# One level of Strassen's algorithm in a channel mixer's up-projection, in fp32, woven with the down-projection of the pair before

## The chip, the cores and the metric

One NeuronCore of a Trainium2 chip; the program runs on that core alone. The metric is the device time of one execution in microseconds, lower is better.

## The reference, cut to what matters

```python
batch, seq, dim = (8, 3008, 256)             # x
d_tok, d_ch = (256, 1536)                    # weights are float64 inputs
# attention part: a filter in the frequency domain along seq
X = np.fft.rfft(x, axis=1)
y = np.fft.irfft(X * (filt_r + 1j * filt_i)[None], n=x.shape[1], axis=1)
# mixer part, on y
xt = y.transpose(0, 2, 1)
h = np.maximum(xt @ w_tok1, 0.0) @ w_tok2    # token mixing
u = y + h.transpose(0, 2, 1)
h2 = np.maximum(u @ w_ch1, 0.0) @ w_ch2      # channel mixing: up (256 -> 1536), relu, down (1536 -> 256)
out = (u + h2).astype(np.float32)
```

The channel mixing is the bulk of the arithmetic. Everything is computed in fp32.

## The kernel before

The filter is done as a two-stage Fourier transform on TensorE: first-stage units (`a_unit`), second-stage units with the multiplication by the filter on VectorE (`b_unit`) and their inverses (`bi_unit`). The filter of the next batch or pair of batches runs beside the mixer of the present one: it is a Python generator, and the mixer's loop calls for one of its steps at every second half pair (every half pair in the first batch). In the traces an engine takes up its work in the order in which it was issued (an instance from ScalarE stands below, at 228 us).

The mixer works on six column blocks of 512 (the last 448) for each batch, and in each on six pairs of hidden tiles; 8 x 6 x 6 = 288 pairs. The down-projection already uses Strassen's algorithm: seven half-width products for eight.

```python
    def hidden(ut, jt, w, hh):
        ps = bank("pg")
        for c in range(DH):
            nc.tensor.matmul(ps[:, 0:w], wc1[:, c, ts(jt, P)], ut[:, c, 0:w],
                             start=(c == 0), stop=(c == DH - 1))
        nc.scalar.activation(out=hh[:, jt % 2, 0:w], in_=ps[:, 0:w], func=AF.Relu)
    def sums(hh, w):
        hw = w // 2
        t = tp.tile([P, 4, 256], FP32, tag="t", name="t")
        v = nc.vector.tensor_tensor
        v(out=t[:, 0:2, 0:hw], in0=hh[:, :, hw:w], in1=hh[:, 0, 0:w].rearrange("p (s n) -> p s n", s=2), op=ALU.subtract)
        v(out=t[:, 2, 0:hw], in0=t[:, 1, 0:hw], in1=hh[:, 0, 0:hw], op=ALU.add)
        v(out=t[:, 3, 0:hw], in0=t[:, 2, 0:hw], in1=hh[:, 1, 0:hw], op=ALU.subtract)
        return t
    def products(m, jp, hh, t, po):
        w = width(m)
        hw = w // 2
        if jp == 0:
            for i in range(4):
                po.append(bank("po%d" % i).rearrange("p (s n) -> p s n", s=2))
        b11, b21, b22 = hh[:, 0, 0:hw], hh[:, 1, 0:hw], hh[:, 1, hw:w]
        t1, t3, t2, t4_ = (t[:, i, 0:hw] for i in range(4))
        todo = ((1, b21), (2, b22)), ((3, t4_), (6, t1)), ((0, b11), (5, t2)), ((4, t3),)
        for i, parts in enumerate(todo):
            for j, (n, mov) in enumerate(parts):
                nc.tensor.matmul(po[i][:, j, 0:hw], wc2[:, jp, n, :], mov, start=(jp == 0 and j == 0),
                                 stop=(jp == JP - 1 and j == len(parts) - 1))
    def finish(b, m, ut, po):
        w = width(m)
        hw = w // 2
        us = ut[:, :, 0:w].rearrange("p d (s n) -> p d s n", s=2)
        u2, u3 = (sp.tile([P, 256], FP32, tag=n, name=n)[:, 0:hw] for n in ("u2", "u3"))
        def add(out, x0, x1):
            nc.vector.tensor_tensor(out=out, in0=x0, in1=x1, op=ALU.add)
        p23, p45, p16, p7 = (v[:, :, 0:hw] for v in po)
        add(us[:, 0], p23, us[:, 0])
        add(us[:, 1], p45, us[:, 1])
        add(us[:, 0, 1], p45[:, 1], us[:, 0, 1])
        nc.scalar.copy(out=u3, in_=p16[:, 0])
        add(u2, p16[:, 1], u3)
        add(us[:, 0, 0], us[:, 0, 0], u3)
        add(u3, p7[:, 0], u2)
        add(us[:, 0, 1], us[:, 0, 1], u2)
        add(us[:, 1], us[:, 1], u3.unsqueeze(1).to_broadcast([P, 2, hw]))
        # ... (cut: two transposes on VectorE, 16 stores)
```

The loop over the pairs:

```python
    def mix(b, next_ready, convert):
        wait = [0]
        pos, hhs, sms = {}, {}, {}
        more = b + 1 < B
        items = [(m, jp) for m in range(MT) for jp in range(JP)]
        n = len(items)
        for i in range(n + 1):
            for half in range(2):
                next(convert, None)
                if i < n:
                    m, jp = items[i]
                    if half == 0:
                        hhs[i] = hp.tile([P, 2, 512], FP32, tag="hh", name="hh")
                    hidden(uts[b, m], 2 * jp + half, width(m), hhs[i])
                    if half == 1:
                        sms[i] = sums(hhs[i], width(m))
                        if m + 1 < MT and jp in (2, 3):
                            u_part(b, m + 1, jp - 2)
                            if jp == 3:
                                wait.append(m + 1)
                        if more and i == n - 2:
                            h1s[b + 1] = token_relu(token_sums(b + 1))
                        if more and i == n - 1:
                            u_part(b + 1, 0, 0)
                elif more and half == 0:
                    u_part(b + 1, 0, 1)
                if half == 1 and i >= 1:
                    m, jp = items[i - 1]
                    products(m, jp, hhs.pop(i - 1), sms.pop(i - 1), pos.setdefault(m, []))
                    if jp == JP - 1:
                        finish(b, m, uts[b, m], pos[m])
                if more and next_ready():
                    for c in wait:
                        t4_load(b + 1, c)
                    wait.clear()
                yield
```

The up-projection of a pair is two `hidden` calls: four full-width matmuls, the activation by ScalarE straight from PSUM. The float64 weights are converted by `rounded`, one ScalarE and five or six VectorE operations for each 128x512 piece. Ten pieces (the "late" ones) are converted by `next(convert, None)` inside the first five pairs of the first batch.

```python
    def rounded(st, n, parts, late=False):
        words = [st.bitcast(t).rearrange("p (n w) -> p n w", w=2)[:, 0:n] for t in (U32, FP32)]
        lo, hi, hi_f = words[0][:, :, 0], words[0][:, :, 1], words[1][:, :, 1]
        if late:
            top = pp.tile([P, 512], FP32, tag="p1", name="top")[:, 0:n]
            rest = pp.tile([P, 512], FP32, tag="p2", name="rest")[:, 0:n]
        else:
            both = hp.tile([P, 2, 512], FP32, tag="hh", name="both")
            top, rest = both[:, 0, 0:n], both[:, 1, 0:n]
        top_i, rest_i = top.bitcast(U32), rest.bitcast(U32)
        nc.scalar.activation(out=top, in_=hi_f, func=AF.Copy, scale=2.0 ** -112)
        nc.vector.tensor_scalar(out=top_i, in0=top_i, scalar1=3, scalar2=None, op0=ALU.logical_shift_left)
        nc.vector.scalar_tensor_tensor(out=top_i, in0=hi, scalar=0x80000000, in1=top_i,
                                       op0=ALU.bitwise_and, op1=ALU.bitwise_or)
        nc.vector.tensor_scalar(out=rest_i, in0=top_i, scalar1=0xFF800000, scalar2=None, op0=ALU.bitwise_and)
        nc.vector.scalar_tensor_tensor(out=rest, in0=lo, scalar=2.0 ** -52, in1=rest, op0=ALU.mult, op1=ALU.mult)
        for src, dst in parts:
            nc.vector.tensor_tensor(out=dst, in0=src(top), in1=src(rest), op=ALU.add)
```

A first-stage unit of the filter uses one PSUM bank, which ScalarE empties:

```python
    def a_unit(b, c, tag):
        ps = bank(tag)
        nc.tensor.matmul(ps, wa, xs.pop((b, c)).rearrange("p a d -> p (a d)"), start=True, stop=True)
        t1 = t1p.tile([P, XC, D], FP32, tag="t1", name="t1")
        nc.scalar.copy(out=t1.rearrange("p a d -> p (a d)"), in_=ps)
        nc.scalar.dma_start(rows_of(z_d, b)[:, ts(c, XC), :], t1)
```

## Time and profile before

| | before |
|---|---|
| median of 4 runs | 2692.7 us (2689.93 to 2696.28) |
| span of the profiled run | 2689.2 us, mean granted clock 0.981 |
| TensorE, VectorE, ScalarE busy | 96%, 45%, 20% |
| first up product at | 191.3 us |

The prediction below shows the lines that carry its reading. A line of the waits view says who waited for whom, then the sum in us, how often, and the longest. A line in order of time gives the start in us, the length, the engine, the source line, the operation, the tiles and shapes, how many records were merged, and in brackets the engine's idle time ahead of it with what ended it. A line that sums up a stretch gives its length, then busy us and record count for PE, PEld, DVE, ACT and POOL, then the clock, the DMA share and GB/s.

### The profile page before, as it was taken

How to read it: one execution, taken by the hardware profiler on the slowest of the kernel's cores; microseconds unless marked ns; L12 is line 12 of the kernel's file. 1: busy time of each engine (PE TensorE's matmuls, PEld its weight loads, DVE VectorE, ACT ScalarE, POOL GpSimd, SP SyncE). 2: the span in 40 equal slices, each digit the busy share in tenths (PEclk: the TensorE clock that was granted, in tenths of full speed). 3: DMA queues.
4: the chain of work that ended last, by engine and by line, in shares of the span. 5: the costliest groups of instructions: out<-in, count | busy, mean ns of one | idle time of the engine just before them, and what ended most of it. 6: DMA issues, size and time to landing. Idle time of an engine off the chain costs nothing.

```text
span 2689.2 us, 26030 instructions
## 1 busy us (share of the span) xinstructions
PE 2594.6 (96%) x9112; PEld 1675.0 (62%) x9112; DVE 1213.7 (45%) x2306; ACT 527.8 (20%) x941; POOL 495.4 (18%) x911
## 2 busy tenths in 40 slices
PE   5769999999999999999999999999999999999997
PEld 1446555766667556676666665676666766676665
DVE  4886477323254655322335456323345343323333
ACT  2223222122211211112221112112122111111111
POOL 3333111112111111211121111211212112112121
PEclk8779999999999999999999999999999999999999
DMA  8665443222222322112232222202222110000000
GB/s 247 182 194 159 127 117 114 86 63 92 89 83 62 88 77 90 33 34 89 75 99 83 66 78 60 82 17 78 82 69 83 53 60 20 20 8 15 8 16 15
DMA packets 166489, 209.41 MB, mean 78 GB/s; under 512 B 35740, under 2 KB 114993, under 8 KB 166358
## 3 DMA queue, kind: packets, MB, share of 16 engines
q1 hardware_dynamic: 92297, 111.04, 13.7%
q0 software_dynamic: 30976, 44.53, 6.6%
q10 hardware_dynamic: 43085, 52.17, 6.0%
q8 instruction: 73, 1.20, 0.2%
q14 instruction: 58, 0.48, 0.1%
HBM read 132.63 MB, written 74.97 MB: 77 GB/s over the span
## 4 chain that ended last, share of the span: by engine, by line
PE 93%; DVE 3%; DMA 2%; issue 1%; POOL 0%; ACT 0%; SPq 0%; ACTq 0%; DVEq 0%; POOLq 0%
PE ps_pg L452 36%; PE ps_po L483 31%; PE ps_acc L440 6%; PE ps_acc L423 5%; PE ps_acc L386 4%; PE ps_b L370 4%; PE ps_acc L445 3%; PE ps_b L338 3%; DMA x<-in_x_dram 1%; DVE both L219 0%; DVE both L223 0%; DVE p L380 0%; DVE p L379 0%; DMA t<-z_tmp 0%; DMA filt<-in_filt_r_dram 0%
## 5 line engine op out<-in xcount | busy, mean ns | idle before, releaser
L452 PE MATMUL ps_pg<-u,wc 128*128 128x512 f32 (+1 forms) x2304 | 1044.4, 583 | 0.0
L518 POOL DMA_DIRECT2D out_dram<-r x757 | 411.4, 552 | 2030.0 <-DVE r L508 2010.1
L452 PEld LDWEIGHTS ps_pg<-u,wc 128*128 128x128 f32 x2304 | 437.2, 190 | 418.8 <-issue 404.2
L454 ACT ACTIVATE hh<-ps_pg 128x512 f32<-128x512 f32 (+1 forms) x576 | 338.9, 588 | 1467.9 <-PE ps_pg L452 1465.6
L467 DVE TENSOR_TENSOR t<-hh 128x512 f32<-128x512 f32 (+1 forms) x288 | 195.9, 680 | 944.6 <-ACT hh L454 943.5
L483 PE MATMUL ps_po<-t,wc 128*128 128x256 f32 (+1 forms) x2304 | 581.1, 375 | 0.0
L483 PEld LDWEIGHTS ps_po<-t,wc 128*128 128x128 f32 x2304 | 437.5, 190 | 49.6
L483 PE MATMUL ps_po<-hh,wc 128*128 128x256 f32 (+1 forms) x1728 | 460.3, 375 | 0.0
L483 PEld LDWEIGHTS ps_po<-hh,wc 128*128 128x128 f32 x1728 | 321.3, 190 | 111.6 <-issue 82.9
L378 DVE TENSOR_TENSOR p<-ps_b,filt 128x512 f32<-128x512 f32 (+1 forms) x144 | 86.0, 597 | 371.0 <-PE ps_b L370 370.3
L440 PE MATMUL ps_acc<-w,h 128*128 128x512 f32 (+1 forms) x384 | 180.5, 592 | 15.9 <-ACT h L429 10.9
L423 PE MATMUL ps_acc<-t,w 128*128 128x256 f32 x768 | 169.6, 383 | 4.3 <-DMA t<-g_tmp 4.3
L386 PE MATMUL ps_acc<-p,wi 128*96 128x512 f32 (+1 forms) x320 | 147.8, 545 | 22.6 <-DVE p L381 12.0
L423 PEld LDWEIGHTS ps_acc<-t,w 128*128 128x128 f32 x768 | 147.6, 192 | 27.9 <-issue 7.8
L370 PE MATMUL ps_b<-t,wb 96*128 96x512 f32 (+1 forms) x288 | 131.4, 538 | 16.2 <-DMA t<-z_tmp 10.7
L440 PEld LDWEIGHTS ps_acc<-w,h 128*128 128x128 f32 x384 | 73.3, 192 | 103.0 <-issue 84.6
L391 ACT COPY t<-ps_acc 96x512 f32<-96x512 f32 (+1 forms) x160 | 79.5, 497 | 262.7 <-PE ps_acc L386 244.2
L445 PEld LDWEIGHTS ps_acc<-wai,t 128*128 128x128 f32 x768 | 102.5, 194 | 45.3 <-issue 45.3
L469 DVE TENSOR_TENSOR t<-t,hh 128x256 f32<-128x256 f32 (+1 forms) x288 | 122.0, 424 | 9.9
L468 DVE TENSOR_TENSOR t<-t,hh 128x256 f32<-128x256 f32 (+1 forms) x288 | 120.7, 419 | 9.8
L493 DVE TENSOR_TENSOR u<-ps_po,u 128x256 f32<-128x256 f32 (+3 forms) x240 | 113.0, 517 | 8.6 <-PE ps_po L483 1.4
L386 PEld LDWEIGHTS ps_acc<-p,wi 128*96 128x96 f32 x320 | 53.3, 175 | 88.7 <-issue 65.3
(59 smaller groups left out, 1147.4 us busy)
## 6 DMA issues: line engine op xcount, KB each, us to landing
z_tmp<-t ACTq DMA_DIRECT2D x96, 256.0 KB
t<-z_tmp SPq DMA_DIRECT2D x128, 192.0 KB
g_tmp<-t ACTq DMA_DIRECT2D x128, 192.0 KB
t<-g_tmp SPq DMA_DIRECT2D x48, 512.0 KB
x<-in_x_dram SPq DMA_DIRECT2D x176, 128.0 KB
out_dram<-r POOLq DMA_DIRECT2D x698, 32.0 KB, 1.8
wb<-wb_t SPq DMA_DIRECT2D x80, 96.0 KB
wi<-wi_t SPq DMA_DIRECT2D x80, 96.0 KB
```

What stands on the lines that cost most here:

```text
L370: nc.tensor.matmul(ps, wbs[k // WC][:, k % WC, :], t2s[k // KC][:, k % KC], start=True, stop=True)
L386: nc.tensor.matmul(ps[0:KR], wis[k // WC][:, k % WC, :], prods.pop(k), start=True, stop=True)
L423: nc.tensor.matmul(acc[:, t, :], w1[:, a, ts(t, P)], t4[b, a // TC4][:, a % TC4, :], start=(a == 0 and t == 0), stop=(a == A - 1 and t == ...
L440: nc.tensor.matmul(ps[:, 0:w], h1[:, t, ts(dh, P)], w2[:, t, ds(m * 512, w)], start=(t == 0), stop=False)
L445: nc.tensor.matmul(ps[:, ds(q * P, n)], t4[b, c][:, r, ts(dh, P)], wai[:, 0:n], start=False, stop=(q == 3))
L452: nc.tensor.matmul(ps[:, 0:w], wc1[:, c, ts(jt, P)], ut[:, c, 0:w], start=(c == 0), stop=(c == DH - 1))
L454: nc.scalar.activation(out=hh[:, jt % 2, 0:w], in_=ps[:, 0:w], func=AF.Relu)
L467: v(out=t[:, 0:2, 0:hw], in0=hh[:, :, hw:w], in1=hh[:, 0, 0:w].rearrange("p (s n) -> p s n", s=2), op=ALU.subtract)
L468: v(out=t[:, 2, 0:hw], in0=t[:, 1, 0:hw], in1=hh[:, 0, 0:hw], op=ALU.add)
L469: v(out=t[:, 3, 0:hw], in0=t[:, 2, 0:hw], in1=hh[:, 1, 0:hw], op=ALU.subtract)
L483: nc.tensor.matmul(po[i][:, j, 0:hw], wc2[:, jp, n, :], mov, start=(jp == 0 and j == 0), stop=(jp == JP - 1 and j == len(parts) - 1))
L518: q.dma_start(rows[g, e, :, ds(h * A + 4 * m, n)], blocks[ts(g, CW), h, e, 0:n])
```

## The change

The intent: give the up-projection the same treatment as the down-projection, seven half-width products for eight. The seven products don't fit in PSUM beside the rest, so they use four half banks twice (four products, then three), and the down-projection of the pair before stands between them on TensorE, to give VectorE time for combining. The sums of the weights are made once, on GpSimd. Room for the larger weights and the sums of u comes from shorter rings of buffers. The finishing of a block is cut into six steps spread over three pairs, and the copy of u out of PSUM moves to ScalarE.

```diff
+XB = 2
...
-    xp = pool("xp", 3)
-    t1p = pool("t1p", 3)
+    xp = pool("xp", XB)
+    t1p = pool("t1p", 2)
...
-    rp = pool("rp", 2)
+    rp = pool("rp", 1)
...
-    wc1 = glob.tile([P, DH, DC], FP32, name="wc1")
+    wc1 = glob.tile([P, JP, 7, P], FP32, name="wc1")
...
+        if c == DH - 1:
+            combine(wc1[:, 2 * q:2 * q + 2])            # five GpSimd operations
...
-        nc.vector.tensor_copy(out=ut[:, dh, 0:w], in_=ps[:, 0:w])
+        nc.scalar.copy(out=ut[:, dh, 0:w], in_=ps[:, 0:w])
...
-    def hidden(ut, jt, w, hh): ...
+    def up_first(jp, ut, vt, w, g):
+        hw = w // 2
+        for ps, n, mov in ((g[0][:, 0], 0, ut[:, 0, 0:hw]), (g[0][:, 1], 5, vt[:, 2, 0:hw]),
+                           (g[1][:, 0], 6, vt[:, 0, 0:hw]), (g[1][:, 1], 4, vt[:, 1, 0:hw])):
+            nc.tensor.matmul(ps[:, 0:hw], wc1[:, jp, n, :], mov, start=True, stop=True)
+        s = sp.tile([P, 3, 256], FP32, tag="s", name="s")[:, :, 0:hw]
+        nc.scalar.copy(out=s[:, 0], in_=g[0][:, 0, 0:hw])
+        return s
+
+    def up_middle(hh, w, g, s):
+        hw = w // 2
+        u2 = hh[:, 2, 0:hw]
+        v(u2, g[0][:, 1, 0:hw], s[:, 0])
+        v(s[:, 1:3], g[1][:, :, 0:hw], u2.unsqueeze(1).to_broadcast([P, 2, hw]))
+
+    def up_last(jp, ut, vt, w, g, s, hh):
+        hw = w // 2
+        for ps, n, mov in ((g[0][:, 0], 1, ut[:, 1, 0:hw]), (g[0][:, 1], 2, ut[:, 1, hw:w]),
+                           (g[1][:, 1], 3, vt[:, 3, 0:hw])):
+            nc.tensor.matmul(ps[:, 0:hw], wc1[:, jp, n, :], mov, start=True, stop=True)
+        h = hh[:, :, 0:hw]
+        for i, add in enumerate((s[:, 0:2], s[:, 2].unsqueeze(1).to_broadcast([P, 2, hw]))):
+            hs = h[:, 2 * i:2 * i + 2]
+            v(hs, g[i][:, :, 0:hw], add)
+            nc.scalar.activation(out=hs, in_=hs, func=AF.Relu)
...
         for i in range(n + 1):
+            now, old = i < n, i >= 1
+            next(convert, None)                          # a late conversion, first batch only
+            if now:
+                ...
+                s = up_first(jp, uts[b, m], vts[b, m], w, g)
+                up_middle(hhs[i], w, g, s)
+            one_step()                                   # a step of a finished block, or of the sums of u
+            if old:
+                ...                                      # sums for the down-projection of pair i - 1
+                down(mo, jo, 0, hhs[i - 1], tts[i - 1], pos.setdefault(mo, []))
+            next(convert, None)                          # a late conversion
+            if now:
+                up_last(jp, uts[b, m], vts[b, m], w, g, s, hhs[i])
+            one_step()
+            loads()
+            yield                                        # a step of the filter stands here
+            if old:
+                down(mo, jo, 1, hhs.pop(i - 1), tts.pop(i - 1), pos[mo])
+                if jo == JP - 1:
+                    todo_v.extend(finish(b, mo, uts[b, mo], pos[mo]))
+                    one_step()
+                    one_step()
+            if now: ...                                  # u of the next block
+            loads()
+            yield                                        # a second one in the first batch
```

## The prediction

> **What bounds the kernel now.** I read the page's first two sections, then the stretches of a batch in mid-kernel, the waits of TensorE, the groups of instructions, and last a few microseconds in order of time.
>
> The page, busy time and the 40 slices (columns: busy us, share of the span, instructions; then tenths busy):
> ```profile
> PE 2594.6 (96%) x9112; PEld 1675.0 (62%) x9112; DVE 1213.7 (45%) x2306; ACT 527.8 (20%) x941; POOL 495.4 (18%) x911
> ...
> PE   5769999999999999999999999999999999999997
> ...
> DVE  4886477323254655322335456323345343323333
> ...
> PEclk8779999999999999999999999999999999999999
> ```
> TensorE is busy in 96% of the span. Its idle time lies in the first three slices (up to about 200 us) and in the last one; from the fourth slice on it is full, at full clock. VectorE and ScalarE have room on average, VectorE least in the early slices (8, 8, 6, 7).
>
> The stretches (columns: length, then busy us and instructions of PE, PEld, DVE, ACT, POOL, the clock, DMA share, GB/s):
> ```profile
> 160.00:202.00 42.00, 26.06 (x75) 14.87 (x74) 34.82 (x73) 11.59 (x20) 18.45 (x34) 0.76 0.52 147
> 202.00:400.00 198.00, 195.26 (x630) 114.53 (x629) 121.10 (x209) 50.13 (x86) 43.00 (x76) 0.99 0.44 133
> 600.00:1000.00 400.00, 400.00 (x1384) 252.29 (x1383) 184.97 (x331) 81.26 (x142) 69.57 (x128) 1.00 0.28 83
> ```
> From 600 us, 400.00 of 400 us are TensorE: after the start every column saved there is time saved, as long as nothing begins to stall it.
>
> The waits of TensorE, the longest ones. All lie in the start; none belongs to the two projections:
> ```profile
> PE ps_acc L440 <- ACT h L429: 10.9, 1, 10.9
> PE ps_b L370 <- DMA t<-z_tmp: 10.7, 4, 8.0
> PE ps_acc L338 <- DMA x<-in_x_dram: 10.6, 3, 8.1
> ```
> Groups (the last two figures before the bar are the union of busy time and the mean of one, which contains the overlapped drain of a matmul, so I don't multiply it):
> ```profile
> L452 PE MATMUL ps_pg<-u,wc 128*128 128x512 f32 (+1 forms) x2304 | 1044.4, 583 | 0.0
> L467 DVE TENSOR_TENSOR t<-hh 128x512 f32<-128x512 f32 (+1 forms) x288 | 195.9, 680 | 944.6 <-ACT hh L454 943.5
> ```
> One fp32 matmul leaves two records: 288 pairs of hidden tiles (8 batches, 6 column blocks, 6 pairs) times 4 matmuls make 1152, and the group has 2304.
>
> What a matmul really costs is the distance from start to start, in the order of time (columns: start us, us, instruction, count):
> ```profile
> 1207.39 1.03 PE L483 MATMUL ps_po<-hh,wc 128*128 128x256 f32 x4
> 1208.26 1.03 PE L483 MATMUL ps_po<-t,wc 128*128 128x256 f32 x4
> ...
> 1212.99 1.88 PE L452 MATMUL ps_pg<-u,wc 128*128 128x512 f32 x4
> 1214.71 0.59 PE L440 MATMUL ps_acc<-w,h 128*128 128x512 f32 x1
> ```
> Four records of 256 columns take 1208.26-1207.39 = 0.87 us, 216 ns each over more such pairs; four of 512 take 1.72 us, 429 each. Taken in the same way from this trace, 448 columns take 376 and 224 take 189.5. Two half-width records cost 432 against 429: halving the width costs almost nothing. That is the down-projection, which already works as the up-projection now shall.
>
> **What the Trainium skill says.** "TensorE: Matmul & The Clock Gate", section "Back-to-back issue gap", gives columns/2.4 + 2.5 ns warm, so 215.7 ns for 512 columns. Here a record takes twice that (429), and the same form holds: twice the width, 1.99 times the time. Same page, "LDWEIGHTS": a load goes by columns alone, and part 2 says that it is pulled ahead under a running matmul. The trace has 190 ns for it, under 216, so 256 columns just hide it; at 224 columns 189.5 is no longer under it, though nothing is visibly lost. "VectorE: DVE Perf Modes", section on the errata, gives (N+151)/0.96 for an fp32 tensor_tensor: 691 ns at 512; the trace has 692 (and 425 at 256). So half-width VectorE work is dear, and a fixed share of every added operation is overhead. "PSUM — Partial Sum Buffer", section "PSUM bank collisions", says two engines may not touch one bank at once, whichever half of it; no run here shows one, but the waits in the built program are by bank, which matters for half banks.
>
> **The change, part by part.**
>
> 1. Matmuls. A pair had 4 x 2 records of 512 = 8 x 429 = 3.43 us; now 7 x 2 of 256 = 14 x 216 = 3.02. In the narrow sixth block 8 x 376 = 3.01 becomes 14 x 189.5 = 2.65. Saved: 240 x 0.41 + 48 x 0.355 = 98 + 17 = 115 us. (Seven eighths of 968 us would be 121; the fixed part per record eats 6.) All of it on the path that sets the end.
>
> 2. VectorE per pair. The three sums for the down-projection stay (0.69 + 0.425 + 0.425). New are one 256-wide and one 512-wide combination out of PSUM, and two 512-wide additions into the hidden tile: 0.42 + 3 x 0.69 = 2.49 us. Per block come three sums of u (1.53 us, 48 times); the two copies of u out of PSUM (2 x 0.69) go to ScalarE. Busy sum: 1214 + 240 x 2.49 + 48 x 2.25 + 48 x 1.53 - 65 = about 1930 us, 74%. Start to start, independent operations overlap by 84 ns and dependent ones lose 34, so a pair costs 0.46 + 0.61 + 0.73 + 0.46 + 0.34 + 0.60 + 0.60 = 3.8 us; a finished block 4.9 us (now cut into six steps over three pairs), the sums of u 1.5.
>
> 3. ScalarE: a 256-wide copy per pair more (0.37), the same two activations, the u copies: far from full.
>
> 4. Latencies within a pair without filter work, in us from its first matmul (matmul results usable 0.2 after the last column, as the trace shows for the activation): first four products until 1.73, three down products until 3.02, last three until 4.32, four down products until 6.05. VectorE: first combination 1.5 to 1.95 (after both matmuls of its bank and the copy), second to 2.6, sums to 4.1, additions 4.1 to 5.4. The bank is wanted again at 3.02 and 3.88; the sums at 4.32. Everything comes a microsecond early, with 2 us of VectorE free. So no regular stall; with a finished block in the way, some 0.2 us per block, 23 such blocks: 5 us.
>
> 5. Pairs beside the filter's middle stage of two batches (one step per pair: 1.72 us TensorE, four dependent VectorE operations 2.74 us): TensorE 7.77 us, VectorE 6.5. Over the four pairs with u sums and a finished block VectorE needs 4 x 6.5 + 6.4 = 32.4 against 31.1: it falls behind by about what the slack holds; 0.3 to 0.5 us per block, 16 blocks: 7 us. The single last batch's filter: 2 us.
>
> 6. The first batch has two filter steps per pair: TensorE 9.5, VectorE 3.8 + 5.5 = 9.3. A finished block and the u sums don't fit, so about 5 us per block are lost, 3 blocks: 14 us.
>
> 7. The first five pairs carry ten conversions of weights (3.2 us of VectorE each): 10.2 us per pair against 7.8 of TensorE, a little more room in two of them; and the combinations of the up weights on GpSimd: 10 us.
>
> 8. Room for all this is taken from buffers: two x tiles for three, so in the start a load that takes 8 us to land is asked for one unit later. The twelve first units, 34 us now, get longer: 8 us (0 to 15). The third t2 buffer is replaced for the first batch, and mid-kernel a unit comes every 8 us or so, so there it costs nothing.
>
> Sum: -115 + 5 + 7 + 2 + 14 + 10 + 8 = -69, so 2692.5 - 69 = 2623; I say 2620.
>
> **The rivals.** (a) VectorE becomes the bound wherever the filter runs. For it: 88% of TensorE's time in step 5, in-order queues, chains PE-ACT-VE-PE inside each pair that the kernel before didn't have. Against it: the totals still fit, and the weaving puts three down products between. If every pair beside the filter's middle stage (about 85) lost 1 us more, 2700; half of that, 2660. (b) The weaving hides all: steps 5 to 7 come to under 10 us, and the time is 2585. For it: token sums (20 us of TensorE without VectorE work per batch) and the u products let VectorE catch up. (c) The 256-wide records run slower in the mixed order, since a wait at a weight load keeps it from being pulled ahead: 190 ns per exposed load, one per pair is 55 us and cancels half. Against it: the down-projection, which also waits on VectorE, shows 216 throughout. (d) Clock: the skill's page ties it to idle windows above 3 us; the start shows 0.76, but stalls in pairs are shorter, so no effect.
>
> **Range and chances.** The floor is 2692 - 115 - a few us, about 2575. My stalls sum to 46, and could be 15 or 85: 2588 to 2662. The 2% mark lies at 2639: it takes 62 us of losses to reach it, against my 46. So faster 0.70, within 2% 0.27, slower 0.03.
>
> **What would show it.** Right: the up-projection has 4032 records, mostly 256 wide, 216 apart; VectorE near 74%; TensorE's waits named by VectorE's additions and combinations, concentrated between 200 and 400 us and nearly none in stretches without filter; ScalarE about 700 us. Wrong if waits appear in every pair of the quiet stretches, if the spacing exceeds 216, if the first 200 us grow by over 20 us, or if VectorE is above 90% in the stretches from 600 us on.

## More of the kernel before

All runs quoted are fast.

One more line from the page before is wanted later, the chain of work that ended last, by engine:

```profile
PE 93%; DVE 3%; DMA 2%; issue 1%; POOL 0%; ACT 0%; SPq 0%; ACTq 0%; DVEq 0%; POOLq 0%
```

Before the change, one can say, TensorE's own work is the time.

## The result, and the profile after

| | before | after |
|---|---|---|
| median of 4 runs | 2692.7 us | 2667.6 us (2664.68 to 2669.7) |
| ratio | | 0.9905, 95% interval 0.9888 to 0.9922 |
| span of the profiled run | 2689.2 us | 2667.9 us |
| TensorE, VectorE, ScalarE busy | 96%, 45%, 20% | 94%, 68%, 25% |

A ratio here, and in every run below, is the mean time of one kernel's fast runs over the mean of the other's fast runs of the same rounds, so it is not quite the ratio of the medians. The kernel is 1% faster, some 25 us, inside 2% and outside the predicted range (2588 to 2662) by 6 us.

The page after, busy time, slices and the chain of work that ended last:

```profile
PE 2511.5 (94%) x10840; PEld 1997.6 (75%) x10840; DVE 1825.9 (68%) x3505; ACT 677.4 (25%) x1325; POOL 503.4 (19%) x926
...
PE   4666999999999999999999999999999999999997
...
DVE  3886588846567688745658588755678586647675
...
PE 71%; DVE 16%; issue 2%; ACT 2%; DMA 0%; SPq 0%; DVEq 0%; POOL 0%; ACTq 0%; POOLq 0%
```

The fourth slice of TensorE, full before, has a 6. VectorE's share of the chain rose from 3% to 16%.

The saving itself came. In a quiet stretch of the fourth batch, in order of time:

```profile
1238.13 1.46 PE L526 MATMUL ps_po<-hh,wc 128*128 128x256 f32 x6
1239.43 1.03 PE L508 MATMUL ps_pg<-u,wc 128*128 128x256 f32 x4
1240.29 0.59 PE L508 MATMUL ps_pg<-v,wc 128*128 128x256 f32 x2
1240.72 1.02 PE L349 MATMUL ps_b<-x,wa 128*128 128x512 f32 x2
```

Six records in 1.30 us and four in 0.86: 216 ns each, in the mixed order too. If I take for every matmul record the plain distance of its width (429 ns for 512 columns, 376, 216, 189.5, 112 and 58 for the narrower ones) the sum over the whole program is 2545.2 us before and 2430.2 after: 115.0 us less, which is what step 1 of the prediction said. That is the prediction's own arithmetic with the records counted; that the chip delivers it is shown below by the run bare.

So the question is where 94 of the 115 went. Sorted by landmarks in the two traces (the first record of the first up product, of the second block, of the second batch, and the end; "loss" is the time after, less the time before reduced by the plain saving of that stretch):

| stretch | before | plain saving | after | loss | predicted loss |
|---|---|---|---|---|---|
| start to the first up product | 191.3 | 0 | 202.3 | 11.0 | 8 (step 8) |
| first six pairs | 51.4 | 2.4 | 83.8 | 34.8 | 10 (step 7) |
| other 30 pairs of the first batch | 312.0 | 11.9 | 317.8 | 17.7 | 14 (step 6) |
| batches two to eight | 2134.5 | 100.6 | 2064.0 | 30.1 | 14 (steps 4, 5) |
| sum | 2689.2 | 114.9 | 2667.9 | 93.6 | 46 |

The largest miss is the first six pairs. The stretch that holds them, before (first fence) and after (second fence):

```profile
191.00:243.00 52.00, 52.00 (x171) 30.71 (x170) 42.89 (x77) 19.19 (x33) 22.67 (x38) 1.00 0.54 166
```
```profile
202.00:286.00 84.00, 60.19 (x205) 40.91 (x205) 57.53 (x101) 22.77 (x42) 31.35 (x53) 0.90 0.34 104
```

Before, TensorE was busy for 52.00 of 52 us, and VectorE's 42.89 lay beside it. After, neither is full: TensorE 60.19 and VectorE 57.53 of 84. That is not an engine that has become the bound; it is engines waiting for each other in turn. TensorE's two longest waits there (view from 186 to 300 us; one of 11.6 us in it lies ahead of the stretch and is left out):

```profile
PE ps_b L349 <- ACT t L351: 15.8, 6, 5.2
PE ps_pg L508 <- DVE hh L470: 6.5, 5, 2.3
```

The longest, 15.8 us, is not for VectorE but for ScalarE, for the copy that empties the filter's bank. One such turn, in order of time over the engines (TensorE, VectorE, ScalarE):

```profile
222.54 1.02 PE L349 MATMUL ps_b<-x,wa 128*128 128x512 f32 x2
...
228.27 1.28 DVE L470 TENSOR_TENSOR hh<-ps_pg,s 128x512 f32<-128x512 f32 x2
...
228.99 1.23 ACT L513 ACTIVATE hh<-hh 128x512 f32<-128x512 f32 x2 [10.50 <-DVE hh L470]
...
230.12 0.57 ACT L351 COPY t<-ps_b 128x512 f32<-128x512 f32 x1
...
230.74 2.08 PE L349 MATMUL ps_b<-x,wa 128*128 128x512 f32 x2 [5.21 <-ACT t L351]
...
234.70 0.43 DVE L220 TENSOR_SCALAR top<-top 128x512 uint32<-128x512 uint32 x1 [5.15 <-ACT top L219]
```

VectorE reaches the two additions of a pair only behind a conversion. ScalarE, which has stood idle for 10.50 us ahead of the activations that need them, does these first and only then the copy that frees the filter's one bank, although that bank has been full since 223.56 us (222.54 + 1.02): what stands behind in the queue doesn't pass. So TensorE waits 5.21 us for a copy that has nothing to do with the pair. Then VectorE stands idle 5.15 us, until ScalarE has got to the start of the next conversion.

A part of the 34.8 us is a slower clock. In the two fences above the granted clock is 1.00 before and 0.90 after. After four of the waits, of 2.2 to 5.2 us, the records of the changed kernel start at twice their plain distance for a while (at 232.61 us, for one, two records of 256 columns take 0.85 us instead of 0.43). There are 27 such records in the six pairs, none in those of the kernel before, and they cost about 6 us (counted from the starts in the trace).

In the later batches the waits are short. TensorE's waits from 600 us to the end:

```profile
PE ps_pg L508 <- DVE hh L470: 7.1, 11, 1.9
PE ps_po L526 <- ACT hh L513: 3.1, 5, 0.7
PE ps_po L526 <- DVE t L470: 1.8, 4, 0.4
```

The three lines sum to 12 us and the whole view to 14.9, where the starts of the records lose 30 (the previous table). A record of 256 columns lasts 379 ns in the profile, and the next starts 216 ns after it, so a wait of less than the difference shows as busy. The Trainium skill says in "Perfetto Trace Analysis", section "Identifying the Most-Contended Engine", that matmul busy time is not a good measure of how close one is to the limit, and this trace agrees. For waits well under a microsecond one has to take start-to-start distances.

### The profile page after: what moved, and what is told of

Same layout as the page of the kernel before. It is cut to its first block, busy times and chain, and to the rows that moved or that the text cites. A ratio compares the mean times of both kernels' runs of the same rounds, so it can differ in the third digit from the quotient of the medians.

```text
span 2667.9 us, 31511 instructions
## 1 busy us (share of the span) xinstructions
PE 2511.5 (94%) x10840; PEld 1997.6 (75%) x10840; DVE 1825.9 (68%) x3505; ACT 677.4 (25%) x1325; POOL 503.4 (19%) x926
## 4 chain that ended last, share of the span: by engine, by line
PE 71%; DVE 16%; issue 2%; ACT 2%; DMA 0%; SPq 0%; DVEq 0%; POOL 0%; ACTq 0%; POOLq 0%
PE ps_po L526 24%; PE ps_pg L492 14%; PE ps_pg L508 11%; PE ps_acc L452 6%; PE ps_acc L435 5%; DVE t L470 3%; PE ps_acc L457 3%; DVE hh L470 3%; PE ps_b L382 2%; PE ps_b L349 2%; PE ps_acc L398 2%; DVE u L470 2%; DVE s L470 2%; DVE p L392 1%; DVE p L391 1%
## 5 line engine op out<-in xcount | busy, mean ns | idle before, releaser
L470 DVE TENSOR_TENSOR hh<-ps_pg,s 128x512 f32<-128x512 f32 (+3 forms) x864 | 482.6, 586 | 639.7 <-ACT s L495 639.7
L513 ACT ACTIVATE hh<-hh 128x512 f32<-128x512 f32 (+1 forms) x576 | 347.9, 621 | 1141.6 <-DVE hh L470 1141.6
L526 PE MATMUL ps_po<-t,wc 128*128 128x256 f32 (+1 forms) x2304 | 535.8, 375 | 3.7 <-DVE t L470 2.4
L526 PEld LDWEIGHTS ps_po<-t,wc 128*128 128x128 f32 x2304 | 434.4, 190 | 128.3 <-issue 50.4
L492 PE MATMUL ps_pg<-v,wc 128*128 128x256 f32 (+1 forms) x1728 | 417.5, 378 | 1.5 <-DVE v L470 1.5
L526 PE MATMUL ps_po<-hh,wc 128*128 128x256 f32 (+1 forms) x1728 | 413.3, 375 | 3.1 <-ACT hh L513 3.1
L492 PEld LDWEIGHTS ps_pg<-v,wc 128*128 128x128 f32 x1728 | 330.5, 192 | 42.5 <-DVE v L470 1.9
L526 PEld LDWEIGHTS ps_po<-hh,wc 128*128 128x128 f32 x1728 | 328.2, 190 | 42.2 <-ACT hh L513 5.1
L508 PE MATMUL ps_pg<-u,wc 128*128 128x256 f32 (+1 forms) x1152 | 294.3, 378 | 16.0 <-DVE hh L470 15.7
L508 PEld LDWEIGHTS ps_pg<-u,wc 128*128 128x128 f32 x1152 | 215.3, 190 | 52.8 <-DVE hh L470 28.6
L470 DVE TENSOR_TENSOR s<-ps_pg,hh 128x512 f32<-128x512 f32 (+1 forms) x288 | 196.1, 681 | 30.0
L452 PE MATMUL ps_acc<-w,h 128*128 128x512 f32 (+1 forms) x384 | 181.7, 596 | 15.8 <-ACT h L441 11.6
L492 PE MATMUL ps_pg<-u,wc 128*128 128x256 f32 (+1 forms) x576 | 172.4, 381 | 0.4 <-DVE hh L470 0.4
L508 PE MATMUL ps_pg<-v,wc 128*128 128x256 f32 (+1 forms) x576 | 169.2, 375 | 0.0
L495 ACT COPY s<-ps_pg 128x256 f32<-128x256 f32 (+1 forms) x288 | 105.8, 367 | 148.6 <-PE ps_pg L492 144.5
```

The source lines that it names most:

```text
L452: nc.tensor.matmul(ps[:, 0:w], h1[:, t, ts(dh, P)], w2[:, t, ds(m * 512, w)], start=(t == 0), stop=False)
L470: nc.vector.tensor_tensor(out=out, in0=in0, in1=in1, op=op)
L492: nc.tensor.matmul(ps[:, 0:hw], wc1[:, jp, n, :], mov, start=True, stop=True)
L495: nc.scalar.copy(out=s[:, 0], in_=g[0][:, 0, 0:hw])
L508: nc.tensor.matmul(ps[:, 0:hw], wc1[:, jp, n, :], mov, start=True, stop=True)
L513: nc.scalar.activation(out=hs, in_=hs, func=AF.Relu)
```

## The experiments

The changed kernel was not run again; each run is compared with the kernel before on its own chip, by the ratio, and with the changed kernel by the stretches of the table above. Ratio 0.9905 is the mark to beat. Where the text speaks of a loss "between 202 and 300 us", it is the sum of start-to-start excess in that window of the clock; the tables here use the landmarks, which don't shift.

Two theories to begin with. A: in the first pairs it is the order in the queues that costs. B: VectorE has too much to do there, in whatever order.

### conv_after: both conversions of a pair moved behind the filter step

```diff
             now, old = i < n, i >= 1
-            next(convert, None)
             if now:
...
-            next(convert, None)
             if now:
                 up_last(...)
...
             yield
+            next(convert, None)
+            next(convert, None)
             if old:
```

> Both weight conversions of a pair are issued behind the filter step in the middle of the pair, not one at its head and one ahead of the last three products. Nothing is removed; only the order in the queues of VectorE and ScalarE changes. The changed kernel loses 35 us of TensorE time between 202 and 300 us (start-to-start distances over the plain 216 or 429 ns). Theory A (order: TensorE waits for combinations and copies that stand behind a conversion in an in-order queue): the loss in that stretch falls to 10 to 15 us, the time to 2643 to 2650. Theory B (load: VectorE simply has too much to do in these pairs, in whatever order): the loss stays near 35, the time within 4 us of 2667.

Measured: 2674.34 us, ratio 0.9922 (0.9910 to 0.9935), correct. The first six pairs took 92.3 us, not less than 83.8. Theory A missed. TensorE's waits in that stretch show why this run doesn't settle it, though:

```profile
PE ps_po L526 <- POOL wc L276: 10.3, 5, 3.3
PE ps_pg L492 <- POOL wc L275: 10.0, 2, 6.4
PE ps_po L526 <- DVE wc L227: 5.0, 2, 3.9
```

The weights are now converted later, GpSimd combines them later, and TensorE waits for them: the edit took away one wait and put another in its place.

### cheap_round: the late conversions leave out the low word

```diff
+        if late:
+            for src, dst in parts:
+                nc.vector.tensor_copy(out=dst, in_=src(top))
+            return
         nc.vector.tensor_scalar(out=rest_i, in0=top_i, scalar1=0xFF800000, ...)
```

> The ten late conversions leave out the low word of the float64 weights (three VectorE operations and a copy instead of five or six; results good to about one part in a million). Some 1.0 to 1.3 us of VectorE less per conversion, 10 to 13 us in all. Theories A and B both: the stretch from 202 to 300 us loses 10 to 15 us less, time 2652 to 2657. Theory C (it is not the conversions: the combinations on GpSimd or the landing of x hold TensorE up there): no change, within 4 us of 2667.

Measured: 2653.83 us, ratio 0.9847 (0.9834 to 0.9861), within the reference's tolerance. First six pairs 69.5 us, 14.3 less than in the changed kernel. The conversions are at the bottom of it, and theory C falls: in the changed kernel no wait of TensorE in these pairs names GpSimd or a load of x. VectorE's busy time in the stretch fell by 12.9 us (57.53 to 44.62), so each microsecond taken from it gave somewhat more than one.

### hold: no filter step beside the conversions

```diff
                 for i, _ in enumerate(mix(b, next_ready, convert)):
-                    if not done and i % len(bs) == 0:
-                        done = next(todo, "end") == "end"
+                    if b == 0 and i < 10:
+                        continue
+                    for _ in range(2 if b == 0 and 12 <= i < 32 and i % 2 == 0 else 1):
+                        if not done and i % len(bs) == 0:
+                            done = next(todo, "end") == "end"
```

> In the first batch no filter step is issued during the first five pairs, while weights are converted; the steps left out are made up, two at a time, in the ten pairs after. The work is the same. Theory A: the 19 us that the filter's first-stage matmuls waited for a ScalarE copy stuck behind activations go away, the other waits stay: 12 to 18 us less, 2650 to 2656. Theory B: VectorE's work in the five pairs is the same and TensorE's filter work only moves to later: within 5 us of 2667.

Measured: 2680.07 us, ratio 0.9942 (0.9929 to 0.9954), correct: slower than either theory said. The six pairs took 70.7 us, but 8.6 us of that difference is filter work that was moved out (ten units of 0.86); the waits are now for VectorE's additions:

```profile
PE ps_pg L492 <- DVE hh L470: 8.5, 4, 3.8
PE ps_pg L508 <- DVE hh L470: 7.3, 4, 2.5
```

The rest of the batch took 339.9 us instead of 317.8, of which the moved work is 8.6. As I read it, the filter units that filled TensorE's waits for nothing now stand where there is less room; no run shows that by itself. So the stuck copy was not the whole cause; where it went away, the wait for the additions came out from behind it.

### filter_first: the filter step ahead of the last three products, in all batches

```diff
             next(convert, None)
+            loads()
+            yield
             if now:
                 up_last(...)
             one_step()
-            loads()
-            yield
             if old:
```

> The filter step of the first half of a pair is issued ahead of the last three up products, in all batches; so its ScalarE copy stands ahead of the two activations. Theory A: in the stretch from 202 to 300 us 10 to 15 us are won; beside the filter's middle stage its four multiplications now stand ahead of the two additions on VectorE and may cost 0 to 8 us over the batches: 2655 to 2662 in all, with the loss after 600 us (30 us now) not smaller. Theory B: within 4 us of 2667 and no change between 202 and 300.

Measured: 2690.05 us, ratio 0.9980 (0.9968 to 0.9993), correct. First six pairs 74.1 us (9.7 less), the other thirty of that batch 304.5 (13.3 less), but batches two to eight 2109.6 us, 45.6 more than in the changed kernel. The expectation had the gain in the six pairs right and the price in the later batches wrong by far. The wait that carries it, over the whole run:

```profile
PE ps_pg L492 <- DVE hh L470: 43.3, 41, 2.8
```

The first products of a pair (L492) wait for the additions of the pair before, which now stand on VectorE behind the filter's four multiplications. In the changed kernel the same wait is 0.4 us in all.

### first_batch: the filter step ahead of the last three products in the first batch only

```diff
             next(convert, None)
+            if b == 0:
+                loads()
+                yield
             if now:
                 up_last(...)
             one_step()
-            loads()
-            yield
+            if b > 0:
+                loads()
+                yield
```

> The filter step stands ahead of the last three up products in the first batch only, where two steps fall on a pair; in the later batches it stands where the changed kernel has it. Run filter_first lost 24 us less than the changed kernel between 202 and 600 us and 45 us more after. If the two are separate effects of the place in the queues, this run keeps the first and is spared the second: 2640 to 2648 us, the loss from 202 to 600 us at 34 to 40 (60 in the changed kernel), after 600 us at 28 to 34. If the gain early only shifts work (or state) into the later batches, the time is 2655 or more.

Measured: 2643.97 us, ratio 0.9813 (0.9800 to 0.9826), correct: as expected. 74.1, 304.5 and 2065.4 us for the three stretches: the gain of the run before without its price. So the order in the queues does cost in the first batch, 23 us in all, which conv_after had hidden. Theory B alone is gone; but 74 us for six pairs is still far from 49, and there the other part of it stands. The stretch:

```profile
198.00:272.00 74.00, 56.68 (x206) 38.81 (x206) 58.24 (x100) 22.30 (x42) 34.07 (x57) 0.93 0.38 121
```

VectorE's busy time is as in the changed kernel (58.24 against 57.53) in 10 us less.

### conv_pre: all ten late conversions before the mixer

```diff
         for _ in range(DH):
             next(convert)
+        for _ in LAST:
+            next(convert, None)
```

> All ten late conversions run before the mixer starts, where TensorE has nothing to do beside them; in the mixer none is left. In the changed kernel the first six pairs take 83.8 us from the first up product to the first of the second block (51.4 before). Theory: the whole excess of these six pairs is the conversions beside the new combinations: 50 to 57 us, while the mixer starts about 32 us later (near 232 us), so that the time changes little: 2663 to 2677. Rival: the excess has another cause in these pairs (GpSimd's combinations, arrival of x): above 70 us for the six pairs, time near 2690.

Measured: 2672.07 us, ratio 0.9921 (0.9909 to 0.9934), correct: as expected. The mixer starts at 235.6 us, and its first six pairs take 55.3 us:

```profile
235.00:291.00 56.00, 51.91 (x208) 38.66 (x207) 26.59 (x49) 17.12 (x32) 5.61 (x10) 0.96 0.31 100
```

28.5 of the 34.8 us lost in the six pairs go with the conversions beside the new combinations. The edit also moves the GpSimd sums that follow each conversion (GpSimd's busy time in the stretch is 5.61 us, 31.35 in the changed kernel), and the clock is 0.96 instead of 0.90; so the 28.5 us are the conversions with all that hangs on them. This is the clearest attribution, and no remedy: before the mixer they cost VectorE's time in full, 33 us.

### x_three: a third tile of x for the first batch

```diff
-        t = xp.tile([P, XC, D], FP32, tag="x", name="x")
+        where, tag = (rp, "r") if b == 0 and c % 3 == 2 else (xp, "x")
+        t = where.tile([P, XC, D], FP32, tag=tag, name="x")
...
-        for u in todo[0:XB]:
+        ahead = XB + first
+        for u in todo[0:ahead]:
             x_load(*u)
...
-            if i + XB < len(todo):
-                x_load(*todo[i + XB])
+            if i + ahead < len(todo):
+                x_load(*todo[i + ahead])
```

> In the first batch a third tile of x is borrowed from the output's buffer, so that x is again asked for three units ahead. The first 202 us lose 120 us of TensorE time in the changed kernel and 109 before. Theory: the difference is the shorter prefetch of x: 8 to 11 us less, the first units end some 10 us earlier, 2656 to 2660. Rival: the start is bound by all that is loaded (82% DMA share in the first 67 us), or by the conversions behind it, so that earlier x only waits elsewhere: within 3 us of 2667.

Measured: 2660.15 us, ratio 0.9875 (0.9861 to 0.9888), correct: at the upper edge of what was expected (2656 to 2660). The third unit of the filter in the changed kernel, and the same in this run:

```profile
20.80 2.05 PE L349 MATMUL ps_acc<-x,wa 128*128 128x512 f32 x2 [7.12 <-DMA x<-in_x_dram]
```
```profile
14.40 2.05 PE L350 MATMUL ps_acc<-x,wa 128*128 128x512 f32 x2 [1.23 <-DMA x<-in_x_dram]
```

The mixer starts at 193.6 us instead of 202.3 (191.3 before). With this start time ranging over 198.3 to 202.3 us in the runs that have the same start, 5 to 9 of the 11 us are the shorter prefetch of x; what the rest is stays open.

### late_steps: the steps of a finished block behind the additions

```diff
                 up_middle(hhs[i], w, g, s)
-            one_step()
             if old:
...
             one_step()
+            one_step()
```

> The steps of a finished block (two per pair) and the sums of u are all issued behind the two additions of a pair, none ahead of the sums for the down-projection. Theory: the 30 us lost after 600 us are waits for the first combination of a pair, delayed on VectorE by these steps of the pair before, and for sums delayed by the step ahead of them. Moving the step behind leaves the first kind and removes the second: loss after 600 us 18 to 26, time 2656 to 2664. Rival: VectorE is late by its total there, so order changes nothing: 30, 2667 plus or minus 3. If the steps now delay the next pair's combination more, the loss grows to 35 to 45.

Measured: 2662.16 us, ratio 0.9876 (0.9863 to 0.9890), correct. In size as expected, but only part of it came where it was expected: the start and the first batch account for 5 us of the difference between the two traces (3 of them in the start, which this edit doesn't touch, so chance), batches two to eight for 2.6. The waits from 600 us on:

```profile
PE ps_pg L508 <- DVE hh L470: 8.5, 18, 1.9
...
PE ps_po L526 <- ACT hh L513: 0.7, 4, 0.2
```

Compared with the changed kernel the waits of the down products (L526) shrank, and those of the last up products (L508) for the first combination grew. In the two windows beside the filter's second stage (800 to 1000 and 1400 to 1600 us) the loss is not smaller but 6.2 us each, against 4.8 and 5.1 in the changed kernel. A small gain, then, whose place fits the theory in part; its size in the later batches doesn't.

### bare: the seven products without their combinations

Wrong results (relative error 0.64).

```diff
-        s = sp.tile([P, 3, 256], FP32, tag="s", name="s")[:, :, 0:hw]
-        nc.scalar.copy(out=s[:, 0], in_=g[0][:, 0, 0:hw])
...
-        v(u2, g[0][:, 1, 0:hw], s[:, 0])
-        v(s[:, 1:3], g[1][:, :, 0:hw], u2.unsqueeze(1).to_broadcast([P, 2, hw]))
...
-        for i, add in enumerate(...):
-            hs = h[:, 2 * i:2 * i + 2]
-            v(hs, g[i][:, :, 0:hw], add)
-            nc.scalar.activation(out=hs, in_=hs, func=AF.Relu)
+        for i in range(2):
+            nc.scalar.activation(out=h[:, 2 * i:2 * i + 2], in_=g[i][:, :, 0:hw], func=AF.Relu)
```

> Wrong results on purpose: the up-projection's seven products run as in the changed kernel, but its combinations on VectorE (three operations and a half, 2.5 us per pair) and the ScalarE copy are left out; ScalarE takes the activation straight from PSUM, as before. If the 92 us that ate the saving are waits for these combinations, apart from the 11 us of the start, then nearly the whole 115 us comes out: 2590 to 2605, loss from 202 to 600 us under 20 and after 600 us under 8. If the seven products themselves or their waits on weights cost it, 2630 or more.

Measured: 2592.34 us, ratio 0.9620 (0.9607 to 0.9633): as expected. Batches two to eight take 2033.7 us, and the time before less the plain saving is 2134.5 - 100.6 = 2033.9. So all 30 us lost there are waits that the combinations on VectorE and ScalarE bring, and the products cost what step 1 said. One stretch:

```profile
600.00:1000.00 400.00, 400.00 (x1734) 317.98 (x1733) 190.74 (x350) 88.78 (x163) 69.28 (x128) 1.00 0.29 87
```

The first six pairs still take 65.1 us, 16 above the plain time. So even without the combinations the new up-projection stands worse beside the conversions than the old one. Its sums of the up weights on GpSimd are one reason that the waits name (5.0 us for converted and combined weights in all); 16 records at twice their plain distance (clock 0.92) are about 3.4 us more; the rest stays open.

### first_and_x and all_three: the experiments that won, together

The edits of first_batch and x_three together, as shown there:

> The two changes first_batch (24 us less) and x_three (8 us less) together. If they act in different places (the first batch's mixer, and the start before it): 2633 to 2638, the mixer's start near 194 us and the first batch at about 379 us.

Measured: 2636.95 us, ratio 0.9788 (0.9774 to 0.9801), correct. The mixer starts at 193.9 us, the first batch takes 380.2: the two edits act in different places and add.

With the edit of late_steps as well:

> first_and_x and also the steps of a finished block behind the additions (late_steps: 6 us less alone). If all add: 2627 to 2633. If late_steps gained in the first batch only by the order that first_batch already changes: as first_and_x, 2633 to 2638.

Measured: 2632.46 us, ratio 0.9772 (0.9759 to 0.9786), correct. This version beats both kernels: 61 us under the kernel before of the same rounds (2693.58) and 35 under the changed one. The three edits are those shown above under first_batch, x_three and late_steps. Its waits for the last up products remain the largest that belong to the mixer:

```profile
PE ps_pg L510 <- DVE hh L472: 18.5, 24, 2.6
```

| run | time | ratio | first product at | first six pairs | rest of batch one | batches two to eight |
|---|---|---|---|---|---|---|
| before | 2692.7 | 1 | 191.3 | 51.4 | 312.0 | 2134.5 |
| changed | 2667.6 | 0.9905 | 202.3 | 83.8 | 317.8 | 2064.0 |
| conv_after | 2674.3 | 0.9922 | 199.5 | 92.3 | 316.7 | 2063.6 |
| cheap_round | 2653.8 | 0.9847 | 200.2 | 69.5 | 315.6 | 2066.8 |
| hold | 2680.1 | 0.9942 | 199.6 | 70.7 | 339.9 | 2065.4 |
| filter_first | 2690.1 | 0.9980 | 199.4 | 74.1 | 304.5 | 2109.6 |
| first_batch | 2644.0 | 0.9813 | 198.3 | 74.1 | 304.5 | 2065.4 |
| conv_pre | 2672.1 | 0.9921 | 235.6 | 55.3 | 315.2 | 2064.0 |
| x_three | 2660.2 | 0.9875 | 193.6 | 85.8 | 315.5 | 2063.9 |
| late_steps | 2662.2 | 0.9876 | 199.1 | 86.1 | 313.7 | 2061.4 |
| bare (wrong) | 2592.3 | 0.9620 | 199.8 | 65.1 | 294.2 | 2033.7 |
| first_and_x | 2637.0 | 0.9788 | 193.9 | 75.7 | 304.5 | 2063.9 |
| all_three | 2632.5 | 0.9772 | 194.0 | 73.0 | 303.8 | 2059.9 |

## Why the prediction was wrong

It was wrong: 2620 was said, 2667.6 came, and 70% of the chance was put on more than 2%. The saving was right. The losses were put at half of what they were (46 against 94), and in the first batch by a mechanism that the runs don't bear out.

- **Step 1** (115 us less on TensorE) was right, and bare shows it on the chip: 100.8 us less over batches two to eight, for a plain saving of 100.6.
- **Steps 2 and 3** were right in size: VectorE was to be busy for about 1930 us and is for 1826 (union of the records), ScalarE for about 700 and is for 677.
- **Step 7 failed.** "10.2 us per pair against 7.8 of TensorE" took the longer of two totals as the length of a pair, as if the longer engine would then be full. Measured, the six pairs lose 34.8 us instead of 10, with VectorE busy for 57.5 of 84 us, and TensorE's longest wait there, 15.8 us, is for a ScalarE copy that the step didn't have. The chain goes from TensorE over VectorE and ScalarE back to TensorE within each pair, and conversions and filter copies stand in the same in-order queues. conv_pre shows that 28.5 us of it go with the conversions in that place; first_batch shows that 9.7 us come back by reordering alone; cheap_round that the loss shrinks by 14.3 us for 12.9 less on VectorE.
- **Steps 4 and 5** were mis-sized: 30.1 us instead of 14 over batches two to eight. bare shows that all of it is the new combinations. The quiet stretches were near the estimate (1.4 us of loss from 1200 to 1400 us); beside the filter's second stage it was 5 us in 200 (800 to 1000 and 1400 to 1600), three times what step 5 allowed. late_steps recovers only 2.6 us of it, so what sets it is not the step ahead of the sums; the waits name the first combination of a pair, and no run took that one away by itself.
- **Step 6** (17.7 us instead of 14) came out in size, but by luck. It said that VectorE's work doesn't fit beside two filter steps per pair; first_batch, with the same work in another order, got 13.3 of the 17.7 back, so most of it was the place in the queues.
- **Step 8** (11.0 instead of 8) held; x_three shows that 5 to 9 of it are the prefetch.
- **Rival (a)**, VectorE as the bound beside the filter, was given too little weight: it named 2660 for half a microsecond per pair, but put the loss beside the filter's second stage, and the larger part lay beside the conversions. Rivals (b) and (c) are out. (d) was dismissed because stalls in pairs would be shorter than 3 us; one of 5.21 us came, the clock fell to 0.90 in the first six pairs, and about 6 us of their loss is that. From 440 us to 2600 it is 1.00.
- Three slips without weight: with steps 4 and 8 kept, (b) comes to 2590 at least and not 2585; stalls of 15 us give 2592 and not 2588; and the three waits shown as TensorE's longest leave out a longer one, for the filter's products (12.0 us, 11.5 of them in the first 202 us).

The range was too narrow for a reason that can be named: steps 5 to 7 took a stall as the difference of two engines' totals less some slack, and here the chain across three in-order queues lost more than that.

## What to carry to other kernels

When a change turns an engine's private work into a chain that goes through two other engines and back, add up not the busy times but, for each in-order queue, what stands ahead of the instruction that the chain needs next; where other streams share the queue (conversions, filter units), their place in it decides. The same reordering can win in one stage and lose more in another, as it did here (23 us won, 46 lost), so it pays to choose the order by stage. And before blaming the added work, run the kernel without it: here that one run confirmed the saving and sized the rest.

## What the Trainium skill lacked or had wrong

- "TensorE: Matmul & The Clock Gate" has no rate for fp32 operands. Here an fp32 matmul leaves two records of 429 ns each at 512 columns and 216 at 256: 858 ns a matmul, four times the page's 215.7. ("FP8 and Floating Point Precision" has four passes for true fp32; that agrees.)
- The same page, section "LDWEIGHTS", gives columns/1.2, which is 107 ns for 128 columns; an fp32 load took 190 ns in these traces, close under the 216 of a half-width matmul, and a matmul record of 224 columns takes 189.5. Whether the load is the limit there isn't shown: the widths 256 and 512 (216 and 429), drawn down in a straight line, give 189 too.
- "VectorE: DVE Perf Modes", section "The DRAIN you can't avoid", says that the next operation starts when the pipe is empty and that one which is not held starts earlier, but not what a dependence costs. Here operations behind a 512-wide addition that don't depend on it mostly started 597 to 610 ns after it, some 83 ns before its record ended, and those that do (the sums t, before the change) 727 ns after it (the median), 34 ns after its end: more than 0.1 us between the two.
- No page that I read says that a wait shorter than a matmul's drain is hidden in the profile's busy time. From 600 us on the waits of TensorE in the profile sum to 14.9 us in the changed kernel (all lines of the view), and the distances between starts lose 30 over batches two to eight.
